# The first block's rows moved on chip, the second bias spread by a transfer, and a new order of layer one's lower parts

## The chip, the cores and the metric

The kernel runs on one core of a Trainium2 chip. The metric is the time of one execution on the device in microseconds (us), as the median of several runs. TensorE (PE in the profile) multiplies matrices, VectorE (DVE), ScalarE (ACT) and GpSimd (POOL) do elementwise work, and transfers (DMA) are issued from the queues of SyncE (SP), ACT and POOL.

## The reference

An image of 4096 positions by 640 channels passes a spectral mixer and then a gated feed-forward layer; a condition vector `c` gives the six modulations. The part that matters here is the start of the mixer:

```python
mod = (_silu(c) @ w_mod).reshape(c.shape[0], 6, 1, -1)
sa, ca, ga, sb, cb, gb = (mod[:, 0], mod[:, 1], mod[:, 2], mod[:, 3], mod[:, 4], mod[:, 5])
h = _layernorm(x, axis=-1) * (1 + ca) + sa
x = x + ga * _A_ref(h, A_w1, A_b1, A_w2, A_b2)
```
```python
Xf = jnp.fft.rfft2(x, axes=(1, 2))
hr = einsum(zr, w1[0]) - einsum(zi, w1[1]) + b1[0]      # and hi; then hr * (hr > 0)
or_ = einsum(hr, w2[0]) - einsum(hi, w2[1]) + b2[0]     # and oi_; then a soft threshold
return jnp.fft.irfft2(Yf, s=(H, W), axes=(1, 2))
```
The einsums are cut here to their operands: four blocks of 160 channels, each with its own weights.

## The kernel before

The Fourier transform of 4096 positions is done as 128 by 32. **Stage a** works on eight tiles `xa0` to `xa7`, each 128 partitions (one factor of the position) by four of the 32 columns by 640 channels. For each tile DVE makes the layer statistics, ACT and DVE normalise in place, TensorE multiplies by the constant `fa` (five matmuls in float32, `dft_a`, line 439), and `evac_a` (lines 446 to 450) copies the result back into the same tile, mostly on ACT. Row `p` of a tile is then a frequency, so the next stage must collect the rows of one group of frequencies out of all eight tiles.

**Stage b** and the layers after it work in eight blocks ("chunks") of frequencies. A block's input `g` has 128 partitions by 2560 numbers. It is collected through scratch memory in HBM: `write_s1` (line 355) writes some of a tile's rows to the scratch `s1`, of which there are four (f = 0 for block 0, f = 1 for block 1, f = 2 and 3 for the others), and `load_g` (lines 308, 311) reads a block. Block 0 is collected in two ways: tiles 0 to 5 through scratch 0, tiles 6 and 7 by `move_g` (line 316), a transfer within on-chip memory that takes 16 rows of 640 numbers (40 KB) to four partitions of `g`; a tile needs four of them. Those of tiles 6 and 7 are issued half on POOL and half on SP.

For a block, TensorE multiplies `g` by a constant (`stage_b`, line 600), ACT and DVE make of it an upper and a lower part (`evac_b`, lines 607 and 608; `evac_r`, lines 630 and 640, for the remaining 32 channels of each group of 160), scaled by `ca1`, which is one plus the second modulation. Then `stage_l1` (line 661) multiplies by w1, `stage_l2` (line 711) by w2, and the bias b2 is added (line 713) from `b2t`, which holds it on all 128 partitions. The weights too are split into an upper part (`weights_high`, lines 281 and 283) and a lower part (`weights_low`, line 286); float32 accuracy is kept by the products of the parts.

b2 reaches all partitions by TensorE: `b2s` has it on its first partition and zeros elsewhere, and three matmuls with a matrix of ones (line 481) spread it; ACT copies the result. After that, `idle(4)` gives TensorE four matmuls without use (line 334).

The order of the work is written out by hand: every engine does its instructions in the order of the program, and so does each queue of transfers. `moves(t)` is what SP issues after tile `t`. Between them the engines wait on semaphores. Transfers issued on SP and ACT share eight semaphores (DMAHW0 to DMAHW7), those on POOL have others (DMASW0 to DMASW7); they are handed out in turn, in an order of the whole program that is fixed when it is built, and an instruction that issues a transfer waits until the transfer before it on its semaphore is complete, if that is not known from elsewhere.

Of the kernel before, what the change touches and what calls it, by code (L numbers as in the profile page):

```python
# [9 lines left out]
OP = mybir.AluOpType  # L10
# [163 lines left out]
def body(tc, x, w1, b1, w2, b2, wg, wu, wd, c, wm, k_fa, k_tb, k_tx, k_bm, k_bx, k_ga, k_ge, k_id, out, dbg=None):  # L174
# [27 lines left out]
    with ExitStack() as top:  # L202
# [35 lines left out]
        with ExitStack() as af:  # L238
# [97 lines left out]
            stx = ExitStack()  # L336
            xp = stx.enter_context(tc.tile_pool(name="xp", bufs=1, side="right"))
            rp = af.enter_context(tc.tile_pool(name="rp", bufs=1))
            b2t = rp.tile([P, 2, NB, BS], F32, name="b2t")
            with tc.tile_pool(name="sp", bufs=1) as sp:  # L340
                xas = []
                xts = {t: xp.tile([P, 4, D], F32, name=f"xa{t}") for t in (1, 2, 3, 0, 4, 5, 6, 7)}

                def load_x(t):
                    xa = xts[t]
                    if t < 3:
                        for i in range(4):
                            nc.sync.dma_start(xa[:, i, :], xv[:, 4 * t + i, :])
                    else:
                        nc.sync.dma_start(xa, xv[:, 4 * t:4 * t + 4, :])  # L350
                    xas.append(xa)


                def write_s1(t, f):
                    nc.sync.dma_start(s1[f][4 * t:4 * t + 4].rearrange("n r d -> r n d"),
                                      xas[t][(slice(0, 64, 4), slice(64, P, 4), slice(2, P, 4), slice(1, P, 2))[f]])

                for t in range(6):
                    load_x(t)
                wm1 = sp.tile([P, 5, D], F32, name="wm1")  # L360
                stats = {}
                pas = {}
                raws = {}


                def moves(t):
                    if t < 6:
                        write_s1(t, 0)
                    if t < 4:
                        write_s1(t, 1)  # L370
                    if t == 0:
                        load_x(6)
                        nc.sync.dma_start(c5, c)
                    elif t == 1:
                        load_x(7)
                        raws[1] = load_weights(sp, w1, "1")
                    elif t == 2:
                        nc.sync.dma_start(wm1, wm[:, 1])
                    elif t == 3:
                        load_tb(0)  # L380
                        nc.sync.dma_start(b1m, b1[:, 0:8].rearrange("p (r b) -> p r b", r=2))
                        nc.sync.dma_start(b1r, b1[0:64, 8:12])
                        nc.sync.dma_start(b2s[0:1], b2.rearrange("r b o -> (r b o)").unsqueeze(0))
                    elif t == 4:

                        load_g(0, (0, 1))
                        raws[2] = load_weights(rp, w2, "2", (0,))
                    elif t == 5:
                        for f in (2, 3):
                            write_s1(1, f)  # L390
                    elif t == 6:

                        for i in range(4):
                            move_g(0, t, i, (pool, nc.sync)[i // 2])
                        load_g(0, (2,))
                    elif t == 7:
                        for i in range(4):
                            move_g(0, t, i, (pool, nc.sync)[i // 2])


                def ln_stats(t):
                    n = 1 if t < 2 else 4
                    for i in range(0, 4, n):
                        mv, rs = layer_stats(lp, xas[t][:, i:i + n, :], n, f"a{t}_{i}")
                        nm = lp.tile([P, 4], F32, tag="nm", bufs=7, name=f"nm{t}_{i}")
                        pool.tensor_tensor(nm[:, :n], mv[:, :, 0], rs, op=OP.mult)
                        pool.tensor_tensor(nm[:, :n], nm[:, :n], mone[:, :n], op=OP.mult)
                        for k in range(n):
                            stats[t, i + k] = (mv[:, k, 0:1], rs[:, k:k + 1], nm[:, k:k + 1])

                def ln_apply(t):
                    xa = xas[t]
                    for i in range(4):
                        mean, rs, nm = stats[t, i]
                        if i >= (4, 2, 2, 3, 2, 3, 2, 1)[t]:
                            dve.tensor_scalar(xa[:, i, :], xa[:, i, :], mean, rs, op0=OP.subtract, op1=OP.mult)
                        else:
                            act.activation(xa[:, i, :], xa[:, i, :], AF.Identity, bias=nm, scale=rs)


                b2s = sp.tile([P, 2 * NB * BS], F32, name="b2s")
                pool.memset(b2s, 0.0)
                acc0 = sp.tile([P, D], F32, name="acc0")
                wx0 = sp.tile([P, P], F32, name="wx0")

                def first_scale(lo, hi):
                    if lo == 0:
                        dve.tensor_scalar(acc0, wm1[:, 0, :], sc[:, 0:1], None, op0=OP.mult)
                    for k in range(max(lo, 1), hi):
                        dve.scalar_tensor_tensor(acc0, wm1[:, k, :], sc[:, k:k + 1], acc0, op0=OP.mult, op1=OP.add)  # L430

                def dft_a(t):

                    xnr = xas[t].rearrange("p a (b e) -> p a b e", b=NB)
                    for n, i in enumerate((0, 1, 2, 3, 4) if t < 7 else (4, 0, 1, 2, 3)):
                        j = 5 * t + n
                        pa = (bank0(j // 4, [P, 512], f"pa{t}_{i}") if j % 4 == 0
                              else ps.tile([P, 512], F32, tag=f"p{j % 4}", name=f"pa{t}_{i}"))
                        mm(pa, fa, xnr[:, i, :, 0:128] if i < 4 else xnr[:, :, :, 128:160], start=True, stop=True)
                        pas[t, i] = pa  # L440

                def evac_a(t):
                    xa = xas[t]
                    for i in range(5):
                        if t > 5 and i % 2:
                            dve.tensor_copy(xa[:, i, 0:512], pas[t, i])
                        elif i == 4:
                            act.activation(xa[:, :, 512:640], pas[t, i].rearrange("p (a e) -> p a e", a=4), AF.Copy)
                        else:
                            act.activation(xa[:, i, 0:512], pas[t, i], AF.Copy)  # L450

                ln_stats(0)
                ln_stats(1)
                ln_apply(0)
                for t in range(8):
                    if t + 2 < 8:
                        ln_stats(t + 2)
                    if t + 1 < 8:
                        ln_apply(t + 1)
                    dft_a(t)  # L460
                    if t == 6:

                        prep1 = prep_weights(raws[1], w1a, w1b, w1c, True)
                        for job in prep1[:6]:
                            weights_high(*job, pool)
                        first_scale(0, 2)
                    evac_a(t)
                    if t == 6:
                        first_scale(2, 5)
                        remainders(acc0, wx0)  # L470
                    if t == 2:
                        act.activation(sc, c5, AF.Silu)
                    moves(t)

                pm1 = columns(acc0, wx0)
                dve.tensor_scalar(ca1, pm1[:, 0:5], 1.0, None, op0=OP.add)

                pbs2 = []
                for n, w in enumerate((512, 512, 256)):
                    pbs2.append(ps.tile([P, 512], F32, tag="p2" if n else "p1", name=f"pb2_{n}"))  # L480
                    mm(pbs2[n][:, :w], ones, b2s[:, 512 * n:512 * n + w], start=True, stop=True)
                idle(4)
                for job in prep1[6:]:
                    weights_high(*job)
                b2v = b2t.rearrange("p r b o -> p (r b o)")
                for n, w in enumerate((512, 512, 256)):
                    act.activation(b2v[:, 512 * n:512 * n + w], pbs2[n][:, :w], AF.Copy)
                for job in prep1:
                    weights_low(*job)
# [3 lines left out]
            for t in (2, 3):  # L493
                for f in (2, 3):
                    write_s1(t, f)
# [2043 lines left out]
```

## Time and profile before

| what | us |
|---|---|
| median of 3 runs | 1415.65 (1414.65 to 1416.2) |
| the profiled execution, its own time | 1411.32 |
| its span, first to last instruction | 1409.5 |
| TensorE busy | 1382.5 |
| DVE, ACT, POOL busy | 1067.8, 765.0, 604.6 |
| last copy of stage a ends (ACT) | 49.94 |
| first matmul of stage b | 55.84 |

The profile page has the busy time of each engine, a row of 40 slices of the span, the chain of work that ended last, and the costliest groups of instructions. Other views give the busy time by stretch, who waited for whom (total, times, longest), the instructions in order of time, and the time from a transfer's issue to its landing. In the order of time a row has start, length, engine, line, operation, output<-inputs and count, and in brackets how long the engine sat idle before it and for whom. `SPq` is SP's queue of transfers; PEld is TensorE's load of weights.

### The profile page before, as it was taken

Reading aid. Unit: us, or ns where it says so; the run is one execution under the profiler, and the core shown is the slowest. Engines: PE = TensorE matmul, PEld = TensorE weight load, DVE = VectorE, ACT = ScalarE, POOL = GpSimd, SP = SyncE. Lnnn points to the kernel's source line nnn. Section 1 sums busy time; section 2 is a strip of 40 time slices with the busy share of each in tenths; the row PEclk is TensorE's granted clock in tenths of the full one; section 3 lists DMA queues with packets and bytes.
Section 4 is the critical chain, followed back from the end, with each engine's and each line's share of the span. In section 5 each row is a group of like instructions: output and inputs, shape, how many; then the busy total and the mean of one; then the engine's idle time right before and its main releaser. Section 6 shows DMA issues by size and latency. Waiting matters only on the chain. (4 is left out here: it accounts for less than half of the span.)

```text
span 1409.5 us, 23754 instructions
## 1 busy us (share of the span) xinstructions
PE 1382.5 (98%) x8410; PEld 1310.7 (93%) x8410; DVE 1067.8 (76%) x1861; ACT 765.0 (54%) x1542; POOL 604.6 (43%) x683
## 2 busy tenths in 40 slices
PE   6899999999999999999999999999999999999998
PEld 2599999967999889899999999999999999999998
DVE  8889888889888888649787668678678757375644
ACT  6879999755555554436454345546164624262341
POOL 5700200157766594326445534447153624042241
PEclk9999999999999999999999999999999999999999
DMA  9876466675998897898877998696998668956634
GB/s 371 310 244 211 157 196 193 203 232 170 327 353 308 308 335 263 293 368 308 308 225 281 375 330 288 236 326 230 375 330 309 217 218 282 350 194 217 199 115 149
DMA packets 171016, 377.34 MB, mean 268 GB/s; under 512 B 22193, under 2 KB 81649, under 8 KB 168882
## 3 DMA queue, kind: packets, MB, share of 16 engines
q1 hardware_dynamic: 161794, 359.28, 73.6%
q0 software_dynamic: 6800, 13.93, 3.1%
q10 hardware_dynamic: 2304, 2.62, 0.5%
q8 instruction: 66, 1.08, 0.3%
q14 instruction: 52, 0.43, 0.1%
HBM read 269.48 MB, written 96.80 MB: 260 GB/s over the span
## 5 line engine op out<-in xcount | busy, mean ns | idle before, releaser
L1442 DVE TENSOR_TENSOR wb<-r,wb 128x768 fp32r<-128x768 f32 (+3 forms) x170 | 170.4, 1013 | 13.5 <-ACT wb L1435 13.3
L2050 PE MATMUL pw<-h,wt 128*128 128x384 f32 x412 | 139.3, 338 | 0.6 <-ACT s_y L2069 0.6
L2052 PE MATMUL pw<-h,wt 128*128 128x384 f32 x412 | 138.3, 336 | 0.0
L2051 PE MATMUL pw<-h,wt 128*128 128x384 f32 x412 | 138.1, 335 | 0.0
L1435 ACT ACTIVATE wb<-r 128x768 fp32r<-128x768 f32 (+3 forms) x168 | 104.5, 639 | 56.3 <-PE pw L2063 41.7
L2351 PE MATMUL pc<-wq,L 128*128 128x320 f32 x846 | 132.7, 309 | 0.9 <-DMA wq<-wqd 0.9
L2110 POOL TENSOR_TENSOR sg<-s_x,sg 128x384 f32<-128x384 f32 x24 | 30.0, 1250 | 234.5 <-DVE s_x L2076 234.5
L2351 PEld LDWEIGHTS pc<-wq,L 128*128 128x128 f32 x846 | 126.3, 188 | 1.1 <-DVE x L2308 1.1
L2130 DVE TENSOR_TENSOR L<-sg,L 128x384 fp32r<-128x384 f32 x144 | 101.0, 725 | 27.7 <-ACT L L2126 27.2
L2069 ACT ACTIVATE s_x<-pw 128x384 f32<-128x384 f32 x52 | 25.6, 492 | 164.2 <-PE pw L2052 162.3
L2050 PE MATMUL pw<-h,wb 128*128 128x384 f32 x312 | 105.0, 336 | 0.0
L2051 PE MATMUL pw<-h,wb 128*128 128x384 f32 x312 | 104.4, 335 | 0.0
L2052 PE MATMUL pw<-h,wb 128*128 128x384 f32 x312 | 104.4, 335 | 0.0
L2121 POOL TENSOR_TENSOR sg<-sg,sg 128x384 f32<-128x384 f32 x72 | 91.9, 1276 | 23.4 <-DVE L L2130 20.0
L1973 PE MATMUL pg<-ht,wb 128*128 128x512 f32 x260 | 101.8, 392 | 0.0
L2351 PE MATMUL pe<-wq,L 128*128 128x320 f32 x648 | 101.7, 309 | 0.0
L1974 PE MATMUL pg<-ht,wb 128*128 128x512 f32 x260 | 101.3, 390 | 0.0
L1975 PE MATMUL pg<-ht,wb 128*128 128x512 f32 x260 | 101.2, 389 | 0.0
L2267 PE MATMUL pd<-wq,a 128*128 128x320 f32 x632 | 96.8, 310 | 0.0
L2351 PEld LDWEIGHTS pe<-wq,L 128*128 128x128 f32 x648 | 96.6, 188 | 0.0
L2267 PEld LDWEIGHTS pd<-wq,a 128*128 128x128 f32 x632 | 93.5, 188 | 0.5
L772 POOL DMA_DIRECT2D s<-co x28 | 15.7, 559 | 175.9 <-ACT co L771 175.9
(317 smaller groups left out, 3914.1 us busy)
## 6 DMA issues: line engine op xcount, KB each, us to landing
wq<-wqd SPq DMA_DIRECT2D x83, 640.0 KB, 6.1
wt<-td SPq DMA_DIRECT2D x103, 512.0 KB, 5.4
hs<-ho SPq DMA_DIRECT2D x52, 512.0 KB, 5.2
h<-hs SPq DMA_DIRECT2D x32, 768.0 KB, 7.9
td<-wt SPq DMA_DIRECT2D x25, 512.0 KB, 6.3
r<-in_B_w_gate_dram SPq DMA_DIRECT2D x24, 384.0 KB, 4.4
r<-in_B_w_up_dram SPq DMA_DIRECT2D x24, 384.0 KB, 4.3
xx<-tt SPq DMA_DIRECT2D x56, 160.0 KB, 3.3
```

Of the source, the lines that this page charges most:

```text
L1435: def high(ks, e=slice(0, c), copy=lambda o, i: act.activation(o, i, AF.Copy)):
L1442: dve.tensor_tensor(wbs[t, n][:, 1, ks, e], raw[t, n][:, ks, e], f32(wbs[t, n][:, 0, ks, e]), op=OP.subtract)
L1973: mm(b, wh, hh, start=(kk == 0), stop=False)
L1974: mm(b, wh, hl, start=False, stop=False)
L1975: mm(b, wl, hh, start=False, stop=(kk == 4))
L2050: mm(b, w(0, kp), a[:, kp, 0], start=start and kp == 0, stop=False, skip_group_check=not start)
L2051: mm(b, w(0, kp), a[:, kp, 1], start=False, stop=False, skip_group_check=not start)
L2052: mm(b, w(1, kp), a[:, kp, 0], start=False, stop=kp == 1, skip_group_check=not start)
L2121: pool.tensor_tensor(o, x, y, op=op)
L2130: dve.tensor_tensor(o[:, 1], raws[j], f32(o[:, 0]), op=OP.subtract)
L2267: mm(b[:, :320], l, m, start=start and i == 0, stop=stop and i == len(s) - 1)
L2351: mm(o[:, :320], ls[q][:, x, k], w[:, q, y], start=start and q == 0 and n == 0, stop=q == 1 and n == 2, skip_group_check=not start)
```

## The change

Block 0 no longer goes through scratch: all eight tiles' rows are moved on chip, four moves a tile, by `moves(t)`; all are issued on SP, except that two of tile 7's four are issued on ACT's queue. POOL issues none. All eight tiles of x are loaded at the start. b2 is spread by one transfer that reads its 1280 numbers for each of the 128 partitions; the memset, the three matmuls and the three copies go, and six matmuls without use stand where four stood. ACT copies one more result of tile 7, DVE one fewer. Of w1's lower parts on DVE, the first six stand ahead of `ca1`; of the other six one stands ahead of block 0's first `evac_b` and five behind its `evac_b` and `evac_r`. The functions from `zs` to `evac_rl` are moved up, `rz` lies in another pool, and the writes and loads for the other blocks stand in the same order as before.

```diff
-                for t in range(6):
+                for t in range(8):
                     load_x(t)
+                load_g(0, ())
...
                 def moves(t):
-                    if t < 6:
-                        write_s1(t, 0)
+                    for i in range(4):
+                        move_g(0, t, i, nc.scalar if t == 7 and i % 2 == 0 else nc.sync)
                     if t < 4:
                         write_s1(t, 1)
                     if t == 0:
-                        load_x(6)
                         nc.sync.dma_start(c5, c)
                     elif t == 1:
-                        load_x(7)
                         raws[1] = load_weights(sp, w1, "1")
...
-                        nc.sync.dma_start(b2s[0:1], b2.rearrange("r b o -> (r b o)").unsqueeze(0))
                     elif t == 4:
-
-                        load_g(0, (0, 1))
+                        for f in (2, 3):
+                            write_s1(1, f)
                         raws[2] = load_weights(rp, w2, "2", (0,))
                     elif t == 5:
-                        for f in (2, 3):
-                            write_s1(1, f)
-                    elif t == 6:
-
-                        for i in range(4):
-                            move_g(0, t, i, (pool, nc.sync)[i // 2])
-                        load_g(0, (2,))
-                    elif t == 7:
-                        for i in range(4):
-                            move_g(0, t, i, (pool, nc.sync)[i // 2])
+                        nc.sync.dma_start(b2t.rearrange("p r b o -> p (r b o)"),
+                                          b2.rearrange("r b o -> (r b o)").unsqueeze(0).to_broadcast([P, 2 * NB * BS]))
...
-                        if t > 5 and i % 2:
+                        if t == 6 and i % 2 or t == 7 and i == 3:
                             dve.tensor_copy(xa[:, i, 0:512], pas[t, i])
...
                 pm1 = columns(acc0, wx0)
-                dve.tensor_scalar(ca1, pm1[:, 0:5], 1.0, None, op0=OP.add)
-
-                pbs2 = []
-                for n, w in enumerate((512, 512, 256)):
-                    pbs2.append(ps.tile([P, 512], F32, tag="p2" if n else "p1", name=f"pb2_{n}"))
-                    mm(pbs2[n][:, :w], ones, b2s[:, 512 * n:512 * n + w], start=True, stop=True)
-                idle(4)
+                idle(6)
                 for job in prep1[6:]:
                     weights_high(*job)
-                b2v = b2t.rearrange("p r b o -> p (r b o)")
-                for n, w in enumerate((512, 512, 256)):
-                    act.activation(b2v[:, 512 * n:512 * n + w], pbs2[n][:, :w], AF.Copy)
-                for job in prep1:
+                for job in prep1[:6]:
                     weights_low(*job)
+                dve.tensor_scalar(ca1, pm1[:, 0:5], 1.0, None, op0=OP.add)
...
+                for b, tag in ((0, None), (4, None), (1, "p2")):
+                    stage_b(0, b, tag)
+                for n in (1, 0):
+                    weights_high(*prep2[n])
+                weights_low(*prep1[6])
+                evac_b(0, 0)
+                evac_r(0, 0)
+                for job in prep1[7:]:
+                    weights_low(*job)
...
-            for b, tag in ((0, None), (4, None), (1, "p2")):
-                stage_b(0, b, tag)
-            for n in (1, 0):
-                weights_high(*prep2[n])
-            for b in range(2):
-                evac_b(0, b)
-                evac_r(0, b)
```

How the change moves instructions is shown at three places; `xa_117`, `xa_119` and `xa_122` are tiles 3, 4 and 7, `g_140` is block 0's input. On SP, from tile 3 on, with the semaphores that each row waits for; in the change:

```order
L316 DMA g_140<-xa_117 4x4x640 [waits DMAHW5_49,Activation_49]
L316 DMA g_140<-xa_117 4x4x640 [waits DMAHW6_49]
L316 DMA g_140<-xa_117 4x4x640 [waits DMAHW0_49]
L316 DMA g_140<-xa_117 4x4x640 [waits DMAHW2_49,DVE_49]
L415 DMA s<-xa_117 16x4x640 [waits DMAHW3_49]
L298 DMA tb_419<-in_k_tb_dram 128x512 [waits DMAHW4_49]
L440 DMA b1m<-in_A_b_dram 128x8 [waits DMAHW5_49]
L441 DMA b1r<-in_A_b_dram 64x4 [waits DMAHW6_49]
L316 DMA g_140<-xa_119 4x4x640 [waits DMAHW7_49,Activation_49]
L316 DMA g_140<-xa_119 4x4x640 [waits DMAHW0_49]
L316 DMA g_140<-xa_119 4x4x640 [waits DMAHW1_49,DVE_49]
```
Where SP issued two writes and four small loads after tile 3 before, it issues four moves, one write and three loads; 7 and 1 are missing from the turn of DMAHW semaphores in tile 3 and stand again in tile 4. On ACT, the end of stage a and the start of w1's upper parts, in the change:

```order
L498 ACTIVATE xa_122<-pa_2_556 128x512 [waits DVE_49,PE_49]
L496 ACTIVATE xa_122<-pa_4_550 128x4x128 [waits PE_49]
L316 DMA g_140<-xa_122 4x4x640 [waits DMAHW7_49,Activation_49]
L316 DMA g_140<-xa_122 4x4x640 [waits DMAHW1_49]
L283 ACTIVATE w1a<-rm_325 128x4x128 [waits DMAHW5_49]
```
Two moves of tile 7 now stand between ACT's last copy and w1's upper parts, on semaphores 7 and 1. On DVE, around the first `evac_b` and `evac_r` of block 0; before:

```order
L286 SCALAR_TENSOR_TENSOR w1c<-rr_321,w1c 128x4x32 [waits Activation_49]
L608 SCALAR_TENSOR_TENSOR z_0_663<-pb_0_646,ca_68,z_0_663 128x2x256 [waits Activation_49]
L640 SCALAR_TENSOR_TENSOR rz_666<-pb_4_651,ca_68,rz_666 32x256 [waits PE_49,Activation_49]
L640 SCALAR_TENSOR_TENSOR rz_666<-pb_4_651,ca_68,rz_666 32x256
L608 SCALAR_TENSOR_TENSOR z_1_671<-pb_1_656,ca_68,z_1_671 128x2x256 [waits Activation_49]
```
and in the change:

```order
L358 SCALAR_TENSOR_TENSOR z_0_657<-pb_0_639,ca_68,z_0_657 128x2x256 [waits Activation_49]
L390 SCALAR_TENSOR_TENSOR rz_660<-pb_4_644,ca_68,rz_660 32x256 [waits PE_49,Activation_49]
L390 SCALAR_TENSOR_TENSOR rz_660<-pb_4_644,ca_68,rz_660 32x256
L286 SCALAR_TENSOR_TENSOR w1b<-rm_325,w1b 128x4x128
L286 SCALAR_TENSOR_TENSOR w1c<-rr_326,w1c 128x4x128
L286 SCALAR_TENSOR_TENSOR w1a<-rm_325,w1a 128x4x32
L286 SCALAR_TENSOR_TENSOR w1b<-rm_325,w1b 128x4x32
L286 SCALAR_TENSOR_TENSOR w1c<-rr_326,w1c 128x4x32
L358 SCALAR_TENSOR_TENSOR z_1_674<-pb_1_649,ca_68,z_1_674 128x2x256 [waits Activation_49]
```
Five lower parts of w1 stand between the first and the second `evac_b` on DVE, where none stood.

386 lines of the change are left out of this document (193 added, 193 removed).

## The prediction

> **What bounds the kernel now.** I read the page's engine shares and its 40 slices first, then busy time by stretch, then who waited for whom up to 76 us.
>
> ```profile
> span 1409.5 us, 23754 instructions
> PE 1382.5 (98%) x8410; PEld 1310.7 (93%) x8410; DVE 1067.8 (76%) x1861; ACT 765.0 (54%) x1542; POOL 604.6 (43%) x683
> PE   6899999999999999999999999999999999999998
> ```
> ```profile
> core 0: us, PE busy (x) PEld busy (x) DVE busy (x) ACT busy (x) POOL busy (x), PEclk, DMA share, GB/s
> 0.00:35.00 35.00, 24.40 (x48) 9.71 (x49) 29.61 (x100) 24.27 (x37) 18.66 (x54) 1.00 0.95 369
> 35.00:70.00 35.00, 30.17 (x146) 19.65 (x144) 30.41 (x58) 29.31 (x57) 27.08 (x27) 1.00 0.88 310
> 70.00:105.00 35.00, 34.80 (x275) 34.83 (x276) 28.07 (x61) 25.69 (x54) 0.00 (x0) 1.00 0.74 252
> 55.80:75.80 20.00, 17.09 (x136) 16.30 (x136) 17.39 (x32) 14.10 (x30) 12.30 (x9) 1.00 0.98 366
> ```
> TensorE is short of work only in the first two slices; from 70 us on it is full (34.80 of 35.00). So this change is worth what it does to the start of the first block: a start later by d ends the program later by about d. What holds that start now:
>
> ```profile
> PE pb L600 <- DMA g<-xa: 1.4, 1, 1.4
> PE pc L711 <- DVE r L691: 1.1, 1, 1.1
> PE pb L600 <- DVE z L608: 0.7, 1, 0.7
> ```
> ```profile
> 49.34 0.60 ACT L448 ACTIVATE xa<-pa 128x512 f32<-128x512 f32 x1 [0.26 <-PE pa L439]
> 50.23 1.13 POOL L316 DMA_DIRECT2D g<-xa  x2 [0.30 <-ACT xa L448]
> 50.76 1.20 SPq L316 DMA_DIRECT2D g<-xa  x2
> 53.36 1.05 PE L334 MATMUL pz<-ones 128*128 128x128 f32 x8
> 55.84 2.92 PE L600 MATMUL pb<-tb,g 128*128 128x128 f32 x24 [1.43 <-DMA g<-xa]
> ```
> The last copy of tile 7 ends at 49.94, its four moves are issued by 52.0, and the first block starts at 55.84, when the last of them is in. The three matmuls of the second bias, their copies and the idle matmuls lie inside this wait: taking them out frees nothing by itself.
>
> **The turn of SP's transfers.** In the change all of tile 0 to 7 goes by moves, 30 of 32 on SP, so SP's queue is the matter. Its waits at the start:
>
> ```profile
> SPq L348 <- DMA xa<-in_A_x_dram: 1.6, 2, 1.0
> SPq L350 <- DMA xa<-in_A_x_dram: 1.4, 3, 0.5
> ```
> These are loads into empty buffers; they can wait for nothing but the semaphore that each transfer shares with the eighth before it. So this turn is kept on the chip: a transfer is issued only when the one before it on its semaphore has landed. In the order of the change the two moves on ACT's queue have taken semaphores 7 and 1 out of SP's turn, early: SP's third move of tile 3 goes on 0, not on 7, and the next user of 7 is SP's first move of tile 4. It must wait until ACT's move of tile **seven** has landed. Behind it on SP stand 17 more transfers ahead of the first block, the last of which is the move without which it can't start; and behind those the rest of w2 and all writes and loads for the second block. This is the step on which the forecast rests.
>
> **When ACT issues its moves.** Its last copy ends at 49.94 now. Ahead of it comes a new delay. The condition c5 is needed by ACT at 30.49:
>
> ```profile
> 29.19 1.28 ACT L472 ACT_TABLE_LOAD   x1
> 30.49 0.21 ACT L472 ACTIVATE sc<-c 128x5 f32<-128x5 f32 x1
> 30.60 1.72 ACT L418 ACTIVATE xa<-xa,nm,rs_a 128x640 f32<-128x640 f32 x2
> 45.05 1.09 ACT L450 ACTIVATE xa<-pa 128x512 f32<-128x512 f32 x2 [0.60 <-PE pa L439]
> ```
> ```profile
> 10.93 0.33 SPq L350 DMA_DIRECT2D xa<-in_A_x_dram  x1
> 19.99 0.52 SPq L373 DMA_DIRECT2D c<-in_c_dram  x1
> 30.43 0.58 SPq L378 DMA_DIRECT2D wm<-in_w_mod_dram  x1
> 42.40 0.97 DVE L428 TENSOR_SCALAR acc<-wm,sc 128x640 f32<-128x640 f32 x1
> ```
> ```profile
> c<-in_c_dram SPq DMA_DIRECT2D x1, 2.5 KB, 8.8
> ```
> ```profile
> xa<-in_A_x_dram SPq DMA_DIRECT2D x1, 1280.0 KB, 13.8
> ```
> ```profile
> DMA packets 122, 1.11 MB, mean 429 GB/s; under 512 B 13, under 2 KB 13, under 8 KB 13
> ```
> ```profile
> wm<-in_w_mod_dram SPq DMA_DIRECT2D x1, 1600.0 KB, 11.0
> ```
> First four starts (of issue, and of DVE's use), then, alone, times from issue to landing in us, and the rate of the queue around 19 us. c5 is issued at 19.99 and is in at 28.8; tile 5 (1280 KB) is issued at 10.93 and is in at 24.7. Now tiles 6 and 7 are queued ahead of c5: 1.31 MB at 429 GB/s is 3.1 us each, so 30.9 for tile 7, then one write of 160 KB (0.4) and four moves. A move of 40 KB costs between its bytes (0.1) and as much as a 160 KB write (0.4), so c5 lands at 31.7 to 32.9. ACT, which is busy without a gap from there to 44.45, falls back by 1.2 to 2.4; I take 2.2, near the dear end, because a move is cut into only 16 rows. The modulation weights wm1 are in at 41.4 now (30.43 + 11.0); behind c5 at 32.7 come eight moves, two writes, w1 and wm1, 3.2 + 0.8 + 3.1 + 3.8, so 43.6. DVE wants them at 42.40, but what stands behind them there, the copies of tile 6, waits for ACT and TensorE until 45.05 + 2.2 anyhow. ACT's moves so go out at 50.0 + 2.2 = 52.2.
>
> [...]
>
> **SP's restart.** A transfer within SBUF on a queue that has drained, from later in the trace, and the issue of small moves:
>
> ```profile
> xx<-tt SPq DMA_DIRECT2D x1, 160.0 KB, 2.9
> ```
> ```profile
> 46.65 1.61 SPq L316 DMA_DIRECT2D g<-xa  x2
> 52.01 0.44 SPq L492 DMA_DIRECT2D rr<-in_A_w_dram  x1
> ```
> ACT's first move lands 2.9 later, at 55.1 (bounds 2.9 and the 4.4 from SP's last issue at 51.4 to the 55.84 above). Then SP issues the waiting move, and 17 more follow at 0.60 (50.76: two in 1.20) to 0.80 (46.65: two in 1.61); at 0.66 the last goes out at 66.3. They carry 14 moves, 960 KB of writes, 640 KB of w2 and 640 KB of b2t, some 11 us of queue at the dear price, so issue and queue keep pace. It lands 3.2 later: the first block starts at **69.5 instead of 55.84, 13.7 later** (bounds 11.6 and 19).
>
> **After the start.** TensorE has stood for 15 us by then. How it runs after a long stand, against later, same matmul:
>
> ```profile
> core 0: us, PE busy (x) PEld busy (x), PEclk, DMA share, GB/s
> 7.90:13.20 5.30, 5.22 (x6) 2.04 (x7) 1.00 1.03 389
> 31.60:36.90 5.30, 5.30 (x13) 2.39 (x14) 1.00 1.04 421
> ```
> Half as many in the same time (the clock column reads 1.00 in both). Later stands, the 1.43 ahead of 55.84 for one, cost nothing of the kind; 15 us is nearer to the 8 us before the first. The 24 matmuls at 55.84 would take twice 2.75; only the first 16 stand before ACT's and DVE's work: +1.1 (0 to 2.75). [...] Last, five of w1's lower parts, which DVE makes now before the first block, stand behind its first z and rz:
>
> ```profile
> 54.53 0.69 DVE L286 SCALAR_TENSOR_TENSOR w1b<-rm,w1b 128x512 fp32r<-128x512 f32 x1
> 56.14 0.28 DVE L286 SCALAR_TENSOR_TENSOR w1c<-rr,w1c 128x128 fp32r<-128x128 f32 x1
> 60.85 0.98 DVE L640 SCALAR_TENSOR_TENSOR rz<-pb,ca,rz 32x256 fp32r<-32x256 f32 x2 [0.23 <-ACT rz L630]
> ```
> From 54.53 to 56.42 that is 1.9; DVE is busy 17.39 of the 20 us after 55.8 and TensorE waits for it there (r, z, above), so all but the 0.23 counts: +1.6. In time for an early start this order would be right; for a late one DVE stands idle before it and pays after.
>
> **Sum.** 13.7 + 1.1 + 1.6 = 16.4 us on the profiled execution of 1411.32; the median shown, 1415.65, lies 4.3 above that, and with the same 16.4 the forecast is 1432. Shorter by nothing: the removed matmuls, the memset on POOL and the three copies on ACT were all covered; what is added on ACT, two issues of about 0.6 ahead of w1's upper parts, is covered by SP's delay and would cost up to 1.2 without it. w2's rest and the second block's loads move with SP by about 14 and keep their place before TensorE.
>
> **The rivals.** (a) ACT's moves don't hold SP, because the shared semaphore is satisfied otherwise on the chip. For it: no wait of one queue for another's transfer in this way can be seen in the trace. Against it: the eighth-before wait is kept to in the five waits above. Then SP goes on at about 46.7 instead of 55.1 with the same 18 issues and its own turn: 8.4 less, 1424. (b) Not slower: the moves land as they are issued, c5 is in time, the write and read-back are really saved; the last move goes out at 50.7 and is in at 53.6, the first block starts 2 us earlier, and w1's five parts take up to 1.6 back: 1413.6 to 1415. It decides only if SP is less than about 3 us behind at tile 7; against it are 63 transfers on SP up to that point where 46 stood, at 0.6 each, in a stretch where the DMA share is 0.95. (c) Worse: the second block's loads fall behind TensorE. It would need SP to lose over 4 us more than the start (tile tb of block 2 lands at about 70 and is used at 74.1): about 1440.
>
> **How the numbers follow.** Forecast 0.78, own range 1427 to 1438 (the bounds of the terms, not all at one end); (a) 0.11; (b) 0.07; (c) 0.04. The range of 1422 to 1438 takes in most of (a) and leaves out (b) and (c). 0.2% (2.8 us) is about what can be told from no change: (b) is mostly within it, so faster 0.03, same 0.05, slower 0.92.
>
> **What would show it.** Right: SP idle from about 45 to 55 us, released by the landing of ACT's move; the second tile row of moves and b2t issued after it; TensorE's wait for g of some 14 us; Silu on ACT at 32 to 33; the first 16 matmuls of stage b at half pace; w1's parts between rz and z on DVE; and from 90 us on every view as before, some 16 us later. Wrong: SP issuing tile 4's moves at 47 (then a), a first block before 56 (then b), or TensorE waiting for the second block's g (then c).

## The result, and the profile after

| | before | after |
|---|---|---|
| median | 1415.93 us (4 runs, 1414.65 to 1418.75) | 1435.85 us (4 runs, 1431.63 to 1436.77) |
| ratio, with its 95% interval | | 1.0132 (1.0107 to 1.0158) |
| the profiled execution | 1411.32 | 1436.43 |
| first matmul of the first block | 55.84 | 73.89 |
| first matmul of layer one's third group | 71.60 | 91.98 |

The change makes the kernel 19.9 us slower. The page of the changed kernel, the lines on TensorE, and busy time by stretch:

```profile
span 1434.7 us, 23758 instructions
PE   6589999999999989999999999999999999999999
PEclk9789999999999999999999999999999999999999
```
```profile
core 0: us, PE busy (x) PEld busy (x) DVE busy (x) ACT busy (x) POOL busy (x), PEclk, DMA share, GB/s
0.00:35.00 35.00, 21.23 (x42) 8.15 (x43) 29.80 (x100) 21.85 (x32) 17.54 (x53) 0.96 0.85 325
35.00:70.00 35.00, 21.39 (x62) 10.37 (x60) 15.99 (x35) 19.58 (x36) 13.31 (x16) 0.79 0.57 186
70.00:105.00 35.00, 28.79 (x202) 27.86 (x203) 22.76 (x44) 20.82 (x45) 8.76 (x8) 0.86 0.97 352
```
The loss lies in the first three slices. From 35 to 70 us the DMA share fell from 0.88 to 0.57 and TensorE's busy time from 30.17 to 21.39: everything waits. What waits, in the order of time on TensorE of the changed kernel:

```profile
33.86 19.81 PE L487 MATMUL pa<-xa,fa 128*128 128x512 f32 x40 [4.09 <-ACT xa L468]
73.89 5.49 PE L350 MATMUL pb<-tb,g 128*128 128x128 f32 x24 [16.81 <-DMA rr<-in_A_w_dram]
91.98 0.51 PE L661 MATMUL pl<-z,w1a 128*128 128x256 f32 x3
```
The last row's matmul is the first of layer one's third group; in the kernel before it stands here:

```profile
71.60 0.52 PE L661 MATMUL pl<-z,w1a 128*128 128x256 f32 x3
```
I use it as the mark behind the start: 20.4 us later now, of which 18.05 are there when the first block begins. (The expectations call the same matmul the second block's first of layer one; by the code it is the third group of block 0.) The 16.81 are put down to the load of rr, which these matmuls don't read; it was issued right behind the last move. By the trace's records of its semaphore that move was in at 73.84, so I read the 16.81 as the wait for g. SP's longest wait (total, times, longest), and its queue in order of time:

```profile
SPq L316 <- DMA g<-xa: 10.7, 4, 8.3
```
```profile
47.66 0.57 SPq L441 DMA_DIRECT2D b1r<-in_A_b_dram  x1
56.63 2.51 SPq L316 DMA_DIRECT2D g<-xa  x4
64.85 4.69 SPq L316 DMA_DIRECT2D g<-xa  x6
69.59 0.44 SPq L531 DMA_DIRECT2D rr<-in_A_w_dram  x1
```
and ACT:

```profile
32.80 0.21 ACT L520 ACTIVATE sc<-c 128x5 f32<-128x5 f32 x1 [2.29 <-DMA c<-in_c_dram]
54.34 1.74 ACTq L316 DMA_DIRECT2D g<-xa  x2
```
The last copy of stage a now ends at 54.31. SP has tile 4's moves next at 48.2 and stands for 8.3 us, released by the landing of a move: ACT's, issued at 54.34, which signals the semaphore that this move of SP waits for. Then its row goes out in one piece from 56.63 to 69.54.

Matching ACT's instructions of the two executions one by one, the lag stays at 20 to 21.7 from 92 us to 500 us. The profiled execution then loses 3 to 4 more between 500 and 550 us, most of it where TensorE waits for gt, and some behind it, where the clock reads 0.50 from 533.6 to 537.0 (in the kernel before it stays at 1.00 there). The waits, first the kernel before, then the changed one:

```profile
PE py L1688 <- DMA gt<-in_k_ga_dram: 1.5, 1, 1.5
```
```profile
PE py L1672 <- DMA gt<-in_k_ga_dram: 3.9, 1, 3.9
```
The larger value comes in some executions and not in others, whatever the edit: 1.4 to 1.9 in ten of the experiments below, 3.9 in experiment 4 and 3.6 in experiment 10. So the 25.1 between the two profiled executions overstates it, and the 20.4 at the mark agrees with the 19.9 of the medians.

### The profile page after: what moved, and what is told of

Read it like the earlier page. It is cut to its first block, busy times and chain, and to the rows that moved or that the text cites. A ratio compares the mean times of both kernels' runs of the same rounds, so it can differ in the third digit from the quotient of the medians.

```text
span 1434.7 us, 23758 instructions
## 1 busy us (share of the span) xinstructions
PE 1386.7 (97%) x8408; PEld 1315.2 (92%) x8408; DVE 1063.2 (74%) x1860; ACT 764.3 (53%) x1540; POOL 598.6 (42%) x678
## 5 line engine op out<-in xcount | busy, mean ns | idle before, releaser
L2105 POOL TENSOR_TENSOR sg<-sg,sg 128x384 f32<-128x384 f32 x72 | 92.1, 1280 | 23.1 <-DVE L L2114 19.6
```

Source lines behind the costliest of these rows:

```text
L2105: pool.tensor_tensor(o, x, y, op=op)
```

## The experiments

Starts are of the first matmul of the first block, marks of the third group's first matmul, both in the profiled execution; the starts of kernels with the same queue of SP differ by up to 1.6 us (experiments 7 and 8; where c5 is late, ACT's wait for it alone is 1.1 to 2.9), so a smaller difference of one start shows nothing. The last column is the difference of the medians to the kernel before run beside it (whose medians were 1412.83 to 1415.93), with the ratio's 95% interval where there are several runs.

| edit | start | mark | us to the kernel before |
|---|---|---|---|
| before | 55.84 | 71.60 | |
| the change | 73.89 | 91.98 | +19.9 (1.0107 to 1.0158) |
| 1 tile 7's moves on SP | 65.64 | 82.96 | +12.3 (1.0059 to 1.0109) |
| 2 c5 loaded early | 69.80 | 87.90 | +15.2 (1.0075 to 1.0131) |
| 3 stage a kept busy | 71.30 | 89.24 | +16.5 (one run) |
| 4 edits 1 and 2 | 64.36 | 82.45 | +12.5 (1.0057 to 1.0108) |
| 5 as 4, shorter row on SP | 60.25 | 79.23 | +6.3 (1.0030 to 1.0083) |
| 6 old scheme, two moves on ACT | 64.00 | 81.92 | +7.0 (one run) |
| 7 old scheme | 56.96 | 75.13 | +2.9 (0.9999 to 1.0028) |
| 8 old scheme, kept busy | 55.40 | 70.96 | +0.2 (0.9997 to 1.0025) |
| 9 busy up to the first block | 72.91 | 89.65 | +18.4 (1.0115 to 1.0146) |
| 10 w1's parts ahead | 73.29 | 88.53 | +20.2 (one run) |
| 11 six moves on POOL | 59.45 | 76.80 | +1.7 (0.9999 to 1.0027) |
| 12 as 11, shorter row on SP | 55.03 | 73.86 | +2.1 (1.0005 to 1.0034) |

**1. Is SP held by ACT's moves?**

```diff
-                        move_g(0, t, i, nc.scalar if t == 7 and i % 2 == 0 else nc.sync)
+                        move_g(0, t, i, nc.sync)
```

> The changed kernel, but tile 7's two moves on ACT's queue are issued on SP too. Nothing else. Theory H (SP is held because its next transfer shares a semaphore with ACT's late move): SP goes on at about 48 instead of 56.63, issues its 20 transfers at 0.72 us each until about 62.5, and the first block starts at 66 to 67 instead of 73.89; about 7 us less than the changed kernel, 1428 to 1429. Rival Q (the transfers themselves are the limit, the hold only shows where they pile up): SP's idle time is merely spread over other waits, the first block starts at 72 to 74, and the time stays within 2 us of 1435.9. Under both theories stage a still ends at 53.7.

SP's queue in this kernel:

```profile
47.97 2.50 SPq L316 DMA_DIRECT2D g<-xa  x4
56.18 6.91 SPq L316 DMA_DIRECT2D g<-xa  x8
```
SP goes on at 47.97 instead of 56.63 and has its last move out at 63.09, though it issues two more; the start comes at 65.64, 8.25 earlier and a little ahead of the 66 to 67 expected. The hold is real, and it was made by two moves on another queue.

**2. What the late c5 costs.** The load of c5 is issued behind tile 5's load:

```diff
                 for t in range(8):
                     load_x(t)
+                    if t == 5:
+                        nc.sync.dma_start(c5, c)
...
-                    if t == 0:
-                        nc.sync.dma_start(c5, c)
-                    elif t == 1:
+                    if t == 1:
```

> The changed kernel, but the load of the condition c5 is issued ahead of the loads of tiles 6 and 7. Theory H with cooling (ACT's 2.3 us wait for c5 made TensorE stand 4.1 us, after which five matmuls ran at half pace for 2.1 us more): both go, stage a ends at 49.3 instead of 53.67, ACT's moves go out at 50 instead of 54.34, SP goes on at 52.3, the first block starts at 69.5; 4.4 less, about 1431.5. Rival: the half pace after the stand has another cause than the stand, then only 2.3 is gained: first block at 71.6, 1433.5. Rival Q (transfers are the limit): first block not before 73.

TensorE in stage a of this kernel, and SP's restart, in order of time:

```profile
31.17 16.88 PE L487 MATMUL pa<-xa,fa 128*128 128x512 f32 x38 [1.81 <-ACT xa L468]
52.40 2.50 SPq L316 DMA_DIRECT2D g<-xa  x4
```
All as worked out for both parts of the delay: start 4.1 earlier, 4.7 less by the medians.

**3. Is half of that TensorE's pace?** The changed kernel, ACT still late, with 17 matmuls without use ahead of the fifth tile's first:

```diff
+                        for _ in range(17 if j == 20 else 0):
+                            mm(pa[:, 0:128], ones, ones, start=True, stop=True)
                         mm(pa, fa, xnr[:, i, :, 0:128] if i < 4 else xnr[:, :, :, 128:160], start=True, stop=True)
```

> The changed kernel with 17 matmuls without use (3.8 us) ahead of stage a's fifth tile, written to the place that this tile's first result overwrites. ACT still waits 2.3 for c5. Theory H with cooling: the first five matmuls of the tile take 0.59 each instead of 1.06, stage a ends at 51.6 instead of 53.67, the first block starts at 71.8 instead of 73.9; 1433 to 1434. Rival (the half pace comes from elsewhere): stage a ends at 53.7 or later, no gain.

TensorE in stage a of this kernel:

```profile
33.58 17.61 PE L489 MATMUL pa<-xa,fa 128*128 128x512 f32 x40
```
The same 40 matmuls take 17.61 instead of 19.81 and the start is 2.6 earlier. So the stand while ACT waited cost 2.3 for the wait and 2.1 for the half pace behind it (the 40 take 17.74 in the kernel before). The second price is not fixed: in experiments 1, 9 and 10, where ACT is late too, the 40 take 19.13, 19.13 and 18.92, 1.2 to 1.4 over the kernel before.

**4. Do the two delays add up?** The edits of experiments 1 and 2 together.

> Both edits together: tile 7's moves all on SP, and c5 loaded ahead of tiles 6 and 7. Theory H: once nothing holds SP, the start is set by SP's own row of 20 issues from 47.7 on, which does not wait for stage a; so the second edit adds little to the first: first block at 65.5 to 66.5, 1427 to 1428.5. If the two delays lie one behind the other also here, they add up: first block at 62, 1424. Not below 1418 by either.

They don't: the start is 64.36, between the two forecasts and 1.3 earlier than in experiment 1, which is within what like kernels differ by, and the medians are the same. Once nothing holds SP, its own row sets the start, and TensorE may end stage a 2.9 us earlier or not.

**5. Is that row a matter of issue or of landing?** As 4, and in `moves` the bias's transfer and two writes stand behind tile 7's moves:

```diff
                     elif t == 4:
-                        for f in (2, 3):
-                            write_s1(1, f)
                         raws[2] = load_weights(rp, w2, "2", (0,))
-                    elif t == 5:
+                    elif t == 7:
                         nc.sync.dma_start(b2t.rearrange("p r b o -> p (r b o)"),
...
+                        for f in (2, 3):
+                            write_s1(1, f)
```

> The kernel with tile 7's moves all on SP and c5 loaded early, in which in addition the bias's transfer and two writes for the later blocks are issued behind tile 7's moves instead of between the moves of tiles 4 to 6: three transfers fewer on SP ahead of the first block. Theory H (what sets the start there is SP's own row, about 0.72 us for each transfer from 46.7 on): the last move is issued at 58.7 instead of 61.0, the first block starts at 62.0 instead of 64.4, and the time is 2 us less than with the two edits alone, about 1424. Rival Q (landing, not issue, is the limit, and 40 KB moves land one behind the other): the start stays at 64 or later, 1426.

SP's last moves and TensorE's start, in order of time:

```profile
50.25 7.85 SPq L316 DMA_DIRECT2D g<-xa  x12
60.25 4.75 PE L350 MATMUL pb<-tb,g 128*128 128x128 f32 x24 [4.85 <-DMA g<-xa]
```
Twelve moves go out at 0.65 each and the last has landed 2.15 behind its issue; the start is 4.1 earlier, where I had expected 2.4: the last issue ends at 58.10 instead of 61.01, 2.9 earlier, and lands 1.2 faster. So most of it is the row of issues, as theory H has it. But the 17 issues from SP's restart at 47.17 on take 0.64 each here and the 20 of experiment 4 took 0.71, and the edit took the 640 KB of the bias out of the row: that the pace of issue and the last landing hang on what is under way beside them is not excluded. At the mark only 3.2 of the 4.1 are left.

**6. Does it happen in the old scheme too?** Block 0 is collected as before (with the new bias transfer, and 16 matmuls without use); one edit:

```diff
                     elif t == 7:
                         for i in range(4):
-                            move_g(0, t, i, (pool, nc.sync)[i // 2])
+                            move_g(0, t, i, (nc.scalar, nc.sync)[i // 2])
```

> The old collection of block 0 (experiment with 20 matmuls without use, here 16), with one edit: the two moves of tile 7 that POOL issued are issued on ACT's queue. In the order of the program one of them has a semaphore whose next user is SP's first move of tile 6. Theory H: SP, which issues that move at 46.7 now, must stand until ACT's move of tile 7 has landed, about 52.3, and five more moves and a read go out behind it: first block at 58 to 59 instead of 55.4, 3 us slower. Rival (no hold between queues; ACT's moves land faster than POOL's): first block at 54 to 55.

A wait of SP, and its queue in order of time:

```profile
SPq L311 <- DMA g<-xa: 10.2, 1, 10.2
```
```profile
41.07 11.34 SPq L311 DMA_DIRECT2D g<-s  x2
```
SP stands for 10.2 us in the middle of two reads of scratch, released by a move within the chip. The start is 8.6 later than in experiment 8, three times what I expected: I had reckoned with one of ACT's two moves only. In the trace the other signals the semaphore for which the second read waits, five transfers ahead of the one that I had named.

**7. Bias and order alone.** The change with the old collection of block 0 (loads, moves and copies of stage a as before; the bias's transfer stands where b2's load stood).

> The changed kernel with the old collection of block 0 (tiles 0 to 5 through scratch, tiles 6 and 7 by moves half on POOL and half on SP, tiles 6 and 7 loaded later) and the old copies of tile 7; the bias by a transfer (in the place of the old load of b2) and the new order of w1's lower parts stay. Theory H: all of the loss lies in the moves and loads, the first block starts at 55 to 56.5 as before, and the time is 1414 to 1418, the same as the kernel before. Rival: the 640 KB of the bias, or w1's parts behind the first block's copies, cost of themselves 1.5 us or more: first block after 57 or a wait of TensorE for w1c of over 1 us, 1418 to 1420.

TensorE's first block:

```profile
56.96 5.46 PE L350 MATMUL pb<-tb,g 128*128 128x128 f32 x24 [4.03 <-DMA rr<-in_A_w_dram]
```
The start is 1.1 later than before, a little behind the 56.5 of theory H, the mark 3.5; by the medians it is at the edge of what can be told. The 24 matmuls take 5.46 where they took 2.92. In the kernel before the three matmuls of the bias and the four without use ran up to 54.41, and TensorE stood for 1.43; now it stands for 4.03.

**8. Is it that stand?** The same with `idle(20)` for `idle(6)`.

> The kernel of the experiment with the old collection of block 0, with 20 instead of 6 matmuls without use ahead of the first block. That experiment lost 3.5 us by 71 us although its first block started only 1.1 later: TensorE stood 4.0 us there, because the three matmuls that spread the bias were gone, and ran its 24 matmuls at half pace. Theory H with cooling: with the stand filled, the 24 take 2.9 again instead of 5.46, and the lag by 72 us falls from 3.5 to 1.0 to 1.5; 1414 to 1415.5. Rival (the lag is due to the new order of w1's parts or to the bias's 640 KB): it stays at 3 or more, 1416 to 1418.

The same row of this kernel:

```profile
55.40 2.92 PE L350 MATMUL pb<-tb,g 128*128 128x128 f32 x24
```
2.92 again, the mark at 70.96, and by the medians no difference to the kernel before. From start to mark it is 15.56, before it was 15.76: in this trace w1's new order costs nothing where the block starts early. The bias's transfer and the order of w1 are the same in 7 and 8, so the lag of 7 is not theirs; but it is the traces that show this, since the intervals of the two overlap.

**9. The same in the change.**

```diff
-                idle(6)
+                idle(78)
```

> The changed kernel with 78 instead of 6 matmuls without use after the columns of ca1, so that TensorE works from 55.5 to 72.7, almost until the first block can start. The start itself does not move: 73.9. Theory H with cooling (a stand makes TensorE run at half pace): the 24 matmuls there take 2.9 instead of 5.49, the copies behind the first 16 are ready 1.7 earlier, and the second block's first matmul of layer one comes 1.7 to 2.4 earlier than 91.98; 1433.5 to 1434.5. By the size in the prediction 1.1 is gained, 1434.8. Rival (the half pace there has another cause than the stand, such as the transfers that run beside it): 5.49 stays, 1435 to 1437.

TensorE's first block:

```profile
72.91 2.94 PE L350 MATMUL pb<-tb,g 128*128 128x128 f32 x24 [0.78 <-DMA g<-xa]
```
From start to mark 16.74 instead of 18.09: the half pace costs 1.35 here. At layer one's second row (the matmuls from w1b) the gain is still 2.7, 3.14 behind the start instead of 5.86; then TensorE stands 0.5 for rz and 1.1 for w1b, and half of it is gone. By the medians 1.5 less, which can't be told from nothing (the intervals overlap).

**10. w1's parts.**

```diff
-                weights_low(*prep1[6])
+                for job in prep1[6:]:
+                    weights_low(*job)
                 evac_b(0, 0)
                 evac_r(0, 0)
-                for job in prep1[7:]:
-                    weights_low(*job)
```

> The changed kernel, but all of w1's lower parts stand ahead of the first block's copies on DVE, as in the kernel before. The first block starts at 73.9 as it did. By the prediction 1.6 is gained behind it (the five parts, 1.9, less a wait of 0.23); by the trace of the change, in which the five parts take from 79.68 to 82.97 beside POOL's work, up to 2.3, all that TensorE stands between 80 and 92. Second block's first matmul of layer one at 89.7 to 90.4 instead of 91.98. Rival: the second copies of the first block are the later ones anyway, under 0.5 is gained.

The mark in this kernel:

```profile
88.53 0.52 PE L660 MATMUL pl<-z,w1a 128*128 128x256 f32 x3
```
From start to mark 15.24 instead of 18.09, 2.85 less and more than the 2.3 that I had put as the most. Not all of it is the order: at layer one's second row, ahead of any wait for w1, this kernel is 0.5 nearer to its start (5.37 instead of 5.86), and the clock rose at 78.0, 4.7 behind the start, where in the change it rose at 79.64, 5.75 behind. So the order costs some 2.4 to 2.85 in this one trace. The one time doesn't show it; this execution is one of those with the long wait for gt.

**11 and 12. Can the on-chip way win?** Experiment 11: c5 early; of tiles 5, 6 and 7 two moves each on POOL's queue; wm1 loaded by POOL's queue; the bias's transfer and two writes behind tile 7's moves; the copies of tile 7 as in the kernel before; `idle(18)`. None on ACT. Part of the edit:

```diff
                     for i in range(4):
-                        move_g(0, t, i, nc.scalar if t == 7 and i % 2 == 0 else nc.sync)
+                        if t < 5 or i > 1:
+                            move_g(0, t, i, nc.sync)
+                    if t > 5:
+                        for u in (5, 6) if t == 6 else (7,):
+                            for i in range(2):
+                                move_g(0, u, i, pool)
...
-                        nc.sync.dma_start(wm1, wm[:, 1])
+                        pool.dma_start(wm1, wm[:, 1])
```

> All of block 0 still moved on chip, c5 loaded early, but SP relieved: of tiles 5, 6 and 7 two moves each are issued on POOL, wm1 is loaded by POOL's queue (so that SP is not held until it lands), the bias's transfer and two writes stand behind tile 7's moves, and 18 instead of 6 matmuls without use keep TensorE busy up to the first block. None on ACT's queue. Theory H: without the hold and with a short row SP has its last move out at 51.5 to 52.5, the first block starts at 55 to 56 as in the kernel before, and the time is within 2 us of it: so moving all rows on chip is no gain in itself, the landing of tile 7's moves (4 us) bounds both. Prediction's rival b: the write and read-back saved are worth 2 us, first block at 53.6, 1.5 to 2 us faster than before. Rival Q (32 small moves are too much for the transfers): first block after 58, over 3 us slower than before.

The first and the last of SP's moves behind tile 3's copies:

```profile
40.75 3.69 SPq L316 DMA_DIRECT2D g<-xa  x4
49.95 4.39 SPq L316 DMA_DIRECT2D g<-xa  x6
```
The start came at 59.45, not at 55 to 56: from 40.75, when tile 3's copies are done, to 54.34 SP issued 19 transfers in a row, and the last landed 5 later. That is where rival Q has the start, though the time is not 3 us longer. Experiment 12 decides between the two: it issues tb, the layer-one biases and the first part of w2 ahead of tile 3's moves, and one more write behind tile 7's, with `idle(17)`.

> The kernel of the experiment in which POOL issues six of the moves, with SP's row shortened once more: the loads of tb, the two layer-one biases and the first part of w2 are issued ahead of tile 3's moves, where SP waits for ACT anyway, and one more write goes behind tile 7's moves. From the end of tile 3's copies (40.7) SP then has 14 moves ahead of the first block where it had 19 transfers. Theory H (SP's issue from 40.7 on set the start at 59.45): the last move is out at 51.5 instead of 54.3 and lands 4 later, the first block starts at 55.5 to 57, and the time is within 2 us of the kernel before, on either side. Prediction's rival b (the saved write and read-back are worth 2 us): first block at 53.6, faster than before by 1.5 to 2. Rival Q (so many 40 KB moves land one behind the other whatever the issue does): first block stays at 59 or later.

SP, TensorE and POOL in order of time, and two waits of TensorE:

```profile
43.35 8.80 SPq L316 DMA_DIRECT2D g<-xa  x14
55.03 2.92 PE L350 MATMUL pb<-tb,g 128*128 128x128 f32 x24
61.17 4.00 POOL L281 TENSOR_SCALAR w2b<-rm 128x640 fp32r<-128x640 f32 x2 [6.72 <-DMA s<-xa]
```
```profile
PE pc L715 <- POOL w2c L571: 1.7, 1, 1.7
PE pc L715 <- POOL w2c L281: 1.2, 1, 1.2
```
Fourteen moves at 0.63 each, and rival Q falls: the first block starts at 55.03. That is 0.8 earlier than in the kernel before, less than the starts of like kernels differ by, so a gain there is not shown. What there may be is paid back at once: the writes that were pushed behind the moves read the tiles of x late, in whose place, by the code, w2's parts are made; POOL waits 6.72 for such a write, TensorE 2.9 for POOL, and in the second of these two waits the clock falls: it reads 0.50 from 70.1 to 76.9. From start to mark it is 18.83, where it was 15.76. 1414.96 against 1412.83: a little slower (1.0005 to 1.0034). None of the twelve beats the kernel before.

## Why the prediction was right or wrong

1411.3 + 16.4, and a median 4.3 above the profiled execution, gave 1432; 1435.85 was measured. At the mark the sum of 16.4 stands against 20.4. The mechanism came as forecast, with its signs: SP idle from 48 to 57, the activation of c5 on ACT at 32.80, the first block at half pace, w1's parts between rz and z on DVE. The terms ahead of the start were too small by 4.4 together.

- **The start decides.** Right: 20.4 at the mark, and no more than 1.3 beyond that up to 500 us.
- **SP is held by ACT's moves through the shared semaphore.** Right, and shown: SP idle from 48.2 to 56.63, taken away by experiment 1, made in the old scheme by experiment 6, and in the trace SP's move waits for the semaphore that ACT's move signals. Rival (a), no hold, falls.
- **"ACT's moves so go out at 50.0 + 2.2 = 52.2."** This step was short by 2.1. ACT's wait for c5 was 2.29, as forecast. But I took the delay as passed on one to one; TensorE, which stood for 4.09 meanwhile, ran at half pace behind it, and stage a lost 4.4 (experiments 2 and 3). I had used the half pace only for the stand ahead of the first block. The 2.1 is the largest of four executions (1.2 to 1.4 in the other three, experiment 3). That a move of 40 KB takes as much of the queue as 160 KB, on which the 2.2 (near the dear end) and the load of the queue in SP's restart rest, was my estimate; no run shows it singly, only the 2.29.
- **SP's restart.** The first landing took 2.3 and not 2.9, the 18 issues 12.9 (0.72 each) and not 11.2, the last landing 4.35 and not 3.2: 2.25 more together. The start so came at 73.89 and not 69.5, 18.05 late, inside the bounds of 11.6 to 19. By experiment 5 the issues are most of it; what made each of them slower than 0.66 was not tested.
- **wm1 at 43.6.** It was in by 46.9, as DVE's row shows; the copies of tile 6 waited for TensorE even so, and nothing came of it.

```profile
46.88 0.55 DVE L476 TENSOR_SCALAR acc<-wm,sc 128x640 f32<-128x640 f32 x1 [4.38 <-DMA wm<-in_w_mod_dram]
49.42 1.29 DVE L494 COPY xa<-pa 128x512 f32<-128x512 f32 x2 [1.06 <-PE pa L487]
```
- **Half pace behind the start, +1.1.** 1.35 by experiment 9. The working of 1.1 is not given: 16 of the 24 matmuls at twice 2.75 would add 1.8. All 24 matmuls were slow, and also the first of layer one.
- **Five lower parts of w1, +1.6.** Too small: 2.4 to 2.85 by experiment 10. They took 3.3 on DVE instead of 1.9, because one of them, 0.68 in the kernel before, took 2.05 beside a part of w2 on POOL. The first two and the last of them on DVE:

```profile
79.68 0.69 DVE L286 SCALAR_TENSOR_TENSOR w1b<-rm,w1b 128x512 fp32r<-128x512 f32 x1
80.29 2.05 DVE L286 SCALAR_TENSOR_TENSOR w1c<-rr,w1c 128x512 fp32r<-128x512 f32 x1
82.69 0.28 DVE L286 SCALAR_TENSOR_TENSOR w1c<-rr,w1c 128x128 fp32r<-128x128 f32 x1
```
From start to mark the change is 2.33 longer than the kernel before, against 2.7 forecast, though the two prices found singly come to 3.75 to 4.2. That the two terms agree so well in sum is partly luck: both were too small, and they overlap, since matmuls that are earlier wait longer for w1's parts (experiment 9). Nor is the kernel before a floor: TensorE stood there for r, z and rz (1.1, 0.7 and 0.5), and experiment 10, where all parts of w1 are made long before the late start, has none of these waits (15.24 against 15.76, with TensorE at half pace). That the order does no harm where the block starts early agrees with experiment 8.
- **"Shorter by nothing."** Half right. Taking the bias's matmuls out frees nothing. But they were not only covered: they kept TensorE busy until 1.43 us before the first block, and in the traces of the old scheme their removal costs 2.4 behind the start (15.76 to 18.17 in experiment 7, 15.56 in 8). In the change this can't be seen, since TensorE stands there for 16.8 us anyway.
- **Rival (b)**, the saved write and read-back as a gain of 2 us at the start: with SP relieved the start is 0.8 earlier (experiment 12), too little to be told from nothing. **Rival (c)**, TensorE waiting for the second block's g: no such wait in the trace.

So 4.0 between 16.4 and 20.4 are 2.1 of half pace in stage a, 2.25 of SP's restart (landings and row), and -0.4 behind the start.

## What to carry to other kernels

Before a transfer is put on a second queue, ask which transfer of the first queue has its semaphore next: a queue is in order, so one late transfer elsewhere holds all that stands behind (here 8.3 us, for a move on ACT's queue). A row of small transfers costs its issues (0.63 to 0.72 us each here), and what is pushed behind it is late for its own users (POOL waited 6.72 in experiment 12). Work on TensorE that is "covered" may be what keeps it at full pace; before taking it out, or making another engine late, look at how long TensorE then stands (behind a stand of 4.03 us in experiment 7 the first 24 matmuls took 5.46, without one in experiment 8 2.92).

## What the runs showed of the hardware that I had not expected

**TensorE's clock changed on a grid of 3.41 us.** In the changed kernel, TensorE by stretch:

```profile
core 0: us, PE busy (x), PEclk, DMA share, GB/s
30.00:32.00 2.00, 0.00 (x0) 0.96 0.25 92
38.00:40.00 2.00, 2.00 (x5) 0.83 0.91 264
58.00:62.00 4.00, 0.00 (x0) 0.65 0.50 183
78.00:80.00 2.00, 2.00 (x13) 0.59 0.92 316
```
Between these the column reads 1.00 or 0.50. (Ahead of the clock's first record, at 13.7 us in the kernel before and 11.4 in the changed one, it reads 1.00 also where the pace is half, as in the prediction's row from 7.90 on.) If it is 0.50 for a part of each of these stretches, it fell at 31.84, rose at 38.68, fell at 59.2 and rose at 79.64; the distances 6.84, 20.5 and 20.4 are 2, 6 and 6 times 3.41, and 3.41 is the length of the one other stretch of this execution at 0.50, from 533.61 to 537.03. A stand need not be as long as that for the clock to fall. In experiment 2, a stand of TensorE, and busy time and clock (third figure behind the stretch's length) around its end:

```profile
51.62 1.75 PE L327 MATMUL pmc<-ones,acc 128*128 128x1 f32 x8 [2.20 <-DVE acc L478]
```
```profile
51.00:52.00 1.00, 0.38 (x3) 0.86 0.13 41
```
2.20 us of standing were followed by the fall at 51.72; the 1.81 in stage a of the same kernel and the 1.43 in the kernel before were not. That the share of work in the 3.41 ahead of a change decides, a guess of mine, would fit these, but experiment 12 does not fit it so simply: there the clock fell at 70.1, and in the 3.41 ahead of that TensorE had stood only 1.2 and 0.5, less than the 1.81. What is counted stays open.

**DVE beside POOL.** A lower part of w1 of 128x128 takes 0.28; in experiment 9 the same form took 1.62 while POOL made a part of w2 (first two rows DVE, last POOL):

```profile
78.60 0.28 DVE L286 SCALAR_TENSOR_TENSOR w1a<-rm,w1a 128x128 fp32r<-128x128 f32 x1
78.81 1.62 DVE L286 SCALAR_TENSOR_TENSOR w1b<-rm,w1b 128x128 fp32r<-128x128 f32 x1
78.71 1.57 POOL L567 TENSOR_TENSOR w2c<-rr,w2c 128x640 fp32r<-128x640 f32 x1
```
DVE's ends 0.15 behind POOL's. In experiment 10 the part that took 2.05 in the change is made while POOL does nothing (first row below), in 0.68. In the kernel before it was POOL that was slow: its part of w2a took 3.11, where the like part of w2b took 1.54 at 61.47, while DVE made five of w1's parts one behind the other (second row):

```profile
57.38 0.68 DVE L286 SCALAR_TENSOR_TENSOR w1c<-rr,w1c 128x512 fp32r<-128x512 f32 x1
54.71 3.11 POOL L528 TENSOR_TENSOR w2a<-rm,w2a 128x640 fp32r<-128x640 f32 x1 [3.35 <-ACT w2a L283]
```
No run changed POOL's work alone, so that the one holds up the other is not shown.
